# Banded attention and a mixture of experts in fp32: the second matrix product of the second pass from eight block products to seven

## The chip, the core and the metric

The kernel runs on one core of a Trainium2 chip. The metric is the device time of one execution in microseconds, the median of several runs. All data are float32. The matrix products use the one-pass float32 form (called F32R in the code) with every operand split into a high part, rounded to that form, and a low part (the rest): a product of two split operands is high x high, high x low and low x high, three matmuls.

## The reference

Attention over 4 batches, 8 heads, 576 positions of 64 values gives x, 2304 tokens of 512 values. Then the part that matters here, a dense mixture of 4 experts:

```python
def _moe_ref(x, domain_probs, w1, w2):          # x 2304x512, w1 4x512x1024, w2 4x1024x512
    p = domain_probs / (domain_probs.sum(-1, keepdims=True) + 1e-09)
    out = np.zeros((N, D), dtype=np.float32)
    for e in range(E):
        h = np.maximum(x @ w1[e], 0.0)
        out += p[:, e:e + 1] * (h @ w2[e])
    return out
```

## The kernel before

The hidden dimension of the experts is cut into 16 units of 256 values (4 of each expert), the tokens into 3 blocks of 768. A visit (u, m) works one unit on one block: the first product (x times the unit's 512 x 256 columns of w1), the relu, the second product (768 x 256 hidden values times the unit's 256 x 512 rows of w2), and an add into the block's accumulator, weighted with the token's share of that expert.

The first pass visits all units on block 0 while attention still makes blocks 1 and 2. The second pass is the list `visits` (lines 597 and 598): unit by unit, blocks 1 and 2, 32 visits. The weights of each unit are loaded again for it (`fetch_w1`, `fetch_w2`) and split again (`w1_split`, `w1_sums`, `w1_late`, `w2_late`; high parts on ScalarE, L130; low parts and differences mostly on GpSimd, L127 and L164 to L170).

The first product (`mm1_a`, `mm1_b`, matmuls at L475) already takes seven block products for a 2 x 2 block matrix (a Strassen form): A11, A12, A22 and S1 to S4 are blocks of w1 and sums of them, B11, B21, B22 and T1 to T4 those of x. A block product is 6 matmuls of 384 columns into one PSUM bank; ScalarE copies and VectorE adds put the four blocks of h together (L512 to L540), then h is split into a high part with relu (ScalarE, L493) and a low part (VectorE, L499).

The second product (`mm2`, matmuls at L579) is the plain one. For each of 6 tiles of 128 tokens it runs 6 matmuls of 512 columns with a block of h as the loaded (stationary) operand and w2 as the moving one. Then VectorE weighs the tile and adds it to the accumulator (L588). Three tiles go behind the opening block product of the next visit, three behind the one after that, so that VectorE and ScalarE work beside PE. In the last visit each tile is sent out (L593), the last one in two halves of 256 columns.

All instructions of an engine run in the order in which they are written. All the loads of weights, keys, queries and values and the outputs stand in one queue, SP's, in order too; a DMA that must wait for its buffer holds up what is behind it. `prepare`, `need` and `step` hand out the splitting work in small pieces between PE's work.

Of the kernel before, what the change touches and what calls it, by code (L numbers as in the profile page):

```python
# [48 lines left out]
def kernel(  # L49
# [30 lines left out]
    fp = ctx.enter_context(tc.tile_pool(name="fp", bufs=1))  # L80
    pools = {}
    wp = ctx.enter_context(tc.tile_pool(name="wp", bufs=1))

    ident = const.tile([128, 128], F32, name="ident")
    eps = const.tile([128, 1], F32, name="eps")
# [13 lines left out]
    w2_op = {}  # L99
    raw1 = {}  # L100
    raw2 = {}

    def fetch_w1(u, part=0):
        e, s = divmod(u % NU, FPE)
# [5 lines left out]
        src = w1[e, :, s * FU:(s + 1) * FU].rearrange("(c p) f -> p c f", p=128)  # L110
        nc.sync.dma_start(out=raw1[u][:, c], in_=src[:, c])

    def fetch_w2(u):
        e, s = divmod(u % NU, FPE)
        r = wp.tile([128, 2, DM], F32, tag="r2", name="r2")
        nc.sync.dma_start(
            out=r, in_=w2[e, s * FU:(s + 1) * FU, :].rearrange("(c p) d -> p c d", p=128)
        )
        raw2[u] = r

    held = []
# [13 lines left out]
    def w1_split(u):  # L135

        r = raw1[u]
        gh = wp.tile([128, 3, 2, 128], F32R, tag="g1h", name="g1h", bufs=2)
        gl = wp.tile([128, 3, 2, 128], F32R, tag="g1l", name="g1l", bufs=2)
        a11, a12 = r[:, 0:2, 0:128], r[:, 2:4, 0:128]  # L140
# [31 lines left out]

    def w1_late(u):
        r = raw1.pop(u)
        gh = wp.tile([128, 4, FU], F32R, tag="g2h", name="g2h")
        gl = wp.tile([128, 4, FU], F32R, tag="g2l", name="g2l")
        for n, c, f in (("S2", 0, 0), ("S1", 2, 128), ("S3", 0, 128), ("S4", 2, 0)):
            v = (slice(None), slice(c, c + 2), slice(f, f + 128))
            split(gh[v], gl[v], r[v], nc.gpsimd if u > 2 else nc.vector)
            a_op[u, n] = (gh[v], gl[v])  # L180
            yield
        if u + 2 <= LAST:
            fetch_w1(u + 2)

    def w2_late(u):
# [7 lines left out]
        if 1 < u < LAST:  # L193
            fetch_w2(u + 1)


    b_op = {}

# [350 lines left out]
    def plain(k, half):  # L549
# [4 lines left out]
        for i in range(2):  # L554
            for c in range(2):
# [2 lines left out]
                    h_out(k, f"{c + 1}{half + 1}", banks[c], 2 if (c, half) == (0, 0) else 1)  # L558
                yield "full"

    def mm2(k, first, last, half, cs=None):
        u, m = k
        e = u // FPE % E
        if first and m not in acc_t:
            if m == NBL - 1:
                pools["late"]()
            acc_t[m] = pools["acc"].tile([128, TB // 128, DM], F32, name=f"acc_{m}")
        for i in range(TH // 128):
            at = half * (TH // 128) + i
            tt = m * (TB // 128) + at  # L570
            acc = acc_t[m][:, at, :]
            cs = cs or (range(2) if half == 0 else (1, 0))
            split_tile = last and k == visits[-1] and half == 0 and i == TH // 128 - 1
            for d in (slice(0, DM // 2), slice(DM // 2, DM)) if split_tile else (slice(0, DM),):
                po = pools["m2"].tile([128, 512], F32, tag="m2", name="m2")[:, d]
                for n, (c, low) in enumerate([(c, low) for low in range(2) for c in cs]):
                    h = h_t[k, f"{c + 1}{half + 1}"][low][:, i * 128:(i + 1) * 128]
                    for x, w in enumerate(w2_op[u, c][:2 - low]):
                        nc.tensor.matmul(  # L579
                            po, h, w[:, d], start=(n == 0 and x == 0), stop=(n == 3)  # L580
                        )
                if first:
                    nc.vector.tensor_scalar(
                        out=acc[:, d], in0=po, scalar1=pn[:, tt, e:e + 1], scalar2=None,
                        op0=ALU.mult,
                    )
                else:
                    nc.vector.scalar_tensor_tensor(  # L588
                        out=acc[:, d], in0=po, scalar=pn[:, tt, e:e + 1], in1=acc[:, d],
                        op0=ALU.mult, op1=ALU.add,  # L590
                    )
                if last:
                    nc.sync.dma_start(out=out[tt * 128:(tt + 1) * 128, d], in_=acc[:, d])  # L593
            yield


    visits = [(u, 0) for u in range(2, NU)]
    visits += [(NU + u, m) for u in range(NU) for m in range(1, NBL)]

    def experts(begin):  # L600

# [31 lines left out]
        prepare(w1_split, 3)  # L633
        prepare(w1_sums, 3)
        prepare(w2_late, 3)
        for i, (u, m) in enumerate(visits):
            blocks = [b for v, b in visits if v == u]
            mine = [v for v in visits if v[1] == m]
            ends = m and (u, m) == mine[0], (u, m) == mine[-1]
            if m == blocks[0]:  # L640
                need(w1_late, u)
            yield from mm1_b((u, m))
            if m == blocks[-1] and u < LAST:
                prepare(w1_late, u + 1)
            if (u, m) == (NU - 1, 0):
# [3 lines left out]
            if m == blocks[-1] and u + 2 <= LAST:  # L649
                prepare(w1_split, u + 2)  # L650
                prepare(w1_sums, u + 2)
            if i + 1 < len(visits):

                need(w1_split, visits[i + 1][0])
                need_x(visits[i + 1][1], ("B11", "B21"))
                opening = mm1_a(visits[i + 1])
                yield next(opening)
            if m == blocks[0]:
                need(w2_late, u)
            yield from mm2((u, m), *ends, 1)  # L660
            if i + 1 < len(visits):
                begin()
                yield from opening
                if visits[i + 1] == (NU - 1, 0):

                    assert "m1" in gate
                    need(x_sums, 5)
                    for n in ("T2", "T1"):
                        for j in (4, 5):
                            prepare(x_part, j, n)  # L670
            yield from mm2((u, m), *ends, 0)
            if m == blocks[-1] and u + 2 <= LAST:
                prepare(w2_late, u + 2)

    queue = []
# [25 lines left out]
    with tc.manual_schedule():  # L703
# [3 lines left out]
        early = ExitStack()  # L707
        xrc = early.enter_context(ExitStack())
        psum = bass.MemoryType.PSUM
        pools["acc"] = fp  # L710
# [49 lines left out]
        def begin():  # L760

            if "over" in gate and "m1" not in gate:
                gate.add("m1")
                early.close()
                pools["x"] = ctx.enter_context(
                    tc.tile_pool(name="x2", bufs=1, side="right", reuse_waits="tile")
                )
                for n, bufs in ("m1", 2), ("m2", 4):
                    pools[n] = ctx.enter_context(
                        tc.tile_pool(name=n, bufs=bufs, space=psum, reuse_waits="tile")  # L770
                    )
                pools["acc"] = pools["x"]
# [31 lines left out]
        def x_over():  # L804
            for of in (queue, later):
                while any(key[0] in (x_part, x_sums) for key, _ in of):
                    step(of)
            xrp.__exit__(None, None, None)
            pools["acc"] = ctx.enter_context(
                tc.tile_pool(name="acc2", bufs=1, reuse_waits="tile")  # L810
            )

        pools["late"] = x_over
        gate = set()

        def pause(what):
# [252 lines left out]
```

## Time and profile before

| | |
|---|---|
| median of 3 runs | 824.52 us (822.99 to 825.04) |
| span of the profiled execution | 821.4 us |
| its own time | not listed apart; the median is 3.1 us above the span |
| granted TensorE clock | 1.000 (mean) |
| PE busy, VectorE busy | 812.7 us, 483.5 us |
| HBM read, written | 53.45 MB, 4.72 MB |

Times in rows are microseconds from the span's start unless marked ns. PE is TensorE's matmul, PEld its weight load, DVE VectorE, ACT ScalarE, POOL GpSimd, SP the engine whose queue issues the DMAs; a q behind a name means the engine's queue. L588 is line 588 of the kernel. A row of instructions says line, engine, operation, output<-inputs, shapes, count, then busy time and mean duration of one in ns, then idle time of the engine just before them and what ended it. Matmuls overlap in the pipeline, so the distance of their starts, not their duration, is what one costs.

### The profile page before, as it was taken

Reading aid. Unit: us, or ns where it says so; the run is one execution under the profiler, and the core shown is the slowest. Engines: PE = TensorE matmul, PEld = TensorE weight load, DVE = VectorE, ACT = ScalarE, POOL = GpSimd, SP = SyncE. Lnnn points to the kernel's source line nnn. Section 1 sums busy time; section 2 is a strip of 40 time slices with the busy share of each in tenths; the row PEclk is TensorE's granted clock in tenths of the full one; section 3 lists DMA queues with packets and bytes.
Section 4 is the critical chain, followed back from the end, with each engine's and each line's share of the span. In section 5 each row is a group of like instructions: output and inputs, shape, how many; then the busy total and the mean of one; then the engine's idle time right before and its main releaser. Section 6 shows DMA issues by size and latency. Waiting matters only on the chain.

```text
span 821.4 us, 15447 instructions
## 1 busy us (share of the span) xinstructions
PE 812.7 (99%) x6162; PEld 720.8 (88%) x6162; DVE 483.5 (59%) x1058; ACT 314.7 (38%) x749; POOL 390.3 (48%) x465
## 2 busy tenths in 40 slices
PE   8999999999999999999999999999999999999998
PEld 5778888888888889889889889889889989989987
DVE  5887557665765777555554554554554554555555
ACT  3554454544455446224223323323323323333321
POOL 4546878786777879334233233233243143153110
PEclk9999999999999999999999999999999999999999
DMA  7764624245211124110010010010010010010003
GB/s 230 230 180 132 193 71 133 83 128 158 91 53 52 52 92 140 35 43 26 26 51 27 26 52 26 26 52 26 27 52 26 26 52 26 27 51 1 1 26 128
DMA packets 46770, 59.15 MB, mean 72 GB/s; under 512 B 2905, under 2 KB 36313, under 8 KB 46699
## 3 DMA queue, kind: packets, MB, share of 16 engines
q1 hardware_dynamic: 46283, 57.75, 22.4%
q8 instruction: 48, 0.79, 0.4%
q10 hardware_dynamic: 416, 0.43, 0.1%
q14 instruction: 23, 0.19, 0.1%
HBM read 53.45 MB, written 4.72 MB: 71 GB/s over the span
## 4 chain that ended last, share of the span: by engine, by line
PE 92%; DVE 4%; DMA 1%; ACT 1%; issue 1%; POOL 0%; SPq 0%; POOLq 0%; DVEq 0%; ACTq 0%
PE m L579 46%; PE m1y L475 24%; PE m1x L475 18%; PE po L389 2%; DMA r<-w 1%; PE sc L300 1%; PE wt L824 1%; PE pt L369 1%; DVE xr L227 1%; DVE acc L588 1%; DVE sm L314 1%; DVE hl L499 0%; DVE su L345 0%; ACT hh L493 0%; DVE su L347 0%
## 5 line engine op out<-in xcount | busy, mean ns | idle before, releaser
L588 DVE SCALAR_TENSOR_TENSOR acc<-m,pn,acc 128x512 f32<-128x512 f32 (+1 forms) x271 | 202.2, 747 | 132.0 <-PE m L579 131.9
L579 PE MATMUL m<-w2h,hh 128*128 128x512 f32 x578 | 227.7, 394 | 0.8 <-DVE acc L588 0.3
L579 PE MATMUL m<-w2l,hh 128*128 128x512 f32 x578 | 225.5, 390 | 0.0
L127 POOL TENSOR_TENSOR g2l<-r,g2h 128x256 fp32r<-128x256 f32 x116 | 85.2, 759 | 235.0 <-PE m L579 212.7
L579 PE MATMUL m<-w2h,hl 128*128 128x512 f32 x578 | 179.0, 390 | 0.0
L493 ACT ACTIVATE hh<-s 128x384 fp32r<-128x384 f32 x92 | 48.3, 526 | 236.3 <-DVE s L516 185.2
L579 PEld LDWEIGHTS m<-w2h,hl 128*128 128x128 f32 x578 | 108.3, 188 | 24.5 <-DVE hl L499 1.0
L579 PEld LDWEIGHTS m<-w2h,hh 128*128 128x128 f32 x578 | 108.5, 188 | 23.2 <-DVE acc L588 2.6
L579 PEld LDWEIGHTS m<-w2l,hh 128*128 128x128 f32 x578 | 108.6, 188 | 19.5
L127 POOL TENSOR_TENSOR g1l<-r,g1h 128x256 fp32r<-128x256 f32 x93 | 70.0, 773 | 65.6 <-ACT g1h L130 65.6
L127 POOL TENSOR_TENSOR w2l<-r,w2h 128x512 fp32r<-128x512 f32 x58 | 75.2, 1315 | 47.1 <-ACT w2h L130 47.1
L535 DVE TENSOR_TENSOR s<-m1y,s 128x384 f32<-128x384 f32 x46 | 25.6, 556 | 93.8 <-PE m1y L475 92.3
L526 ACT ACTIVATE u<-m1y 128x384 f32<-128x384 f32 x46 | 22.6, 492 | 146.0 <-PE m1y L475 146.0
L499 DVE SCALAR_TENSOR_TENSOR hl<-s,hh 128x384 fp32r<-128x384 f32 x92 | 55.3, 601 | 27.7 <-ACT hh L493 27.5
L475 PE MATMUL m1y<-xh_T,g2h 128*128 128x384 f32 x152 | 51.9, 341 | 0.0
L475 PE MATMUL m1y<-xl_T,g2h 128*128 128x384 f32 x152 | 51.2, 337 | 0.0
L475 PE MATMUL m1y<-xh_T,g2l 128*128 128x384 f32 x152 | 51.0, 336 | 0.0
L130 ACT ACTIVATE g2h<-r 128x256 fp32r<-128x256 f32 x120 | 42.2, 407 | 0.8 <-POOL r L168 0.8
L475 PE MATMUL m1x<-xh_B,g2h 128*128 128x384 f32 x124 | 41.7, 337 | 0.0
L475 PE MATMUL m1x<-xl_B,g2h 128*128 128x384 f32 x124 | 41.7, 336 | 0.0
L475 PE MATMUL m1x<-xh_B,g2l 128*128 128x384 f32 x124 | 41.4, 334 | 0.0
L130 ACT ACTIVATE w2h<-r 128x512 fp32r<-128x512 f32 x64 | 38.3, 622 | 4.6 <-DMA r<-w 4.6
(133 smaller groups left out, 1477.2 us busy)
## 6 DMA issues: line engine op xcount, KB each, us to landing
r<-w SPq DMA_DIRECT2D x63, 512.0 KB, 3.3
v_s<-vw SPq DMA_DIRECT2D x48, 192.0 KB, 4.6
k_s<-kT SPq DMA_DIRECT2D x23, 224.0 KB, 4.8
q_s<-qT SPq DMA_DIRECT2D x24, 192.0 KB, 4.7
out<-acc SPq DMA_DIRECT2D x17, 256.0 KB, 2.0
r<-w SPq DMA_DIRECT2D x2, 256.0 KB, 4.3
out<-acc SPq DMA_DIRECT2D x2, 128.0 KB, 1.9
k_s<-kT ACTq DMA_DIRECT2D x1, 224.0 KB, 3.7
```

What stands on the lines that cost most here:

```text
L127: lo_eng.tensor_tensor(out=lo, in0=src, in1=hi.bitcast(F32), op=ALU.subtract)
L130: nc.scalar.activation(out=hi, in_=src, func=AF.Copy)
L227: nc.vector.tensor_tensor(out=quarter(i, d), in0=quarter(i, a), in1=quarter(i, b), op=ALU.subtract)
L300: nc.tensor.matmul(banks[swap][o:o + QB, i * KB:(i + 1) * KB], q_s[h, c0:c0 + QB], k_s[h, c0:c0 + KB], start=True, stop=True, skip_group_c ...
L389: nc.tensor.matmul(po[k][64 * j:64 * j + 64, o:o + QB], v_s[rows, j, 2 * i + half, :], ts_[rows, c:c + QB], start=True, stop=True,)
L475: nc.tensor.matmul(bank, w[:, k], x[:, k], start=(first and k == 0 and i == 0), stop=(last and k == 1 and i == 2), skip_group_check=True,)
L493: nc.scalar.activation(out=hi, in_=src, func=AF.Relu)
L499: nc.vector.scalar_tensor_tensor(out=lo, in0=src, scalar=0.0, in1=hi.bitcast(F32), op0=ALU.max, op1=ALU.subtract)
L526: nc.scalar.activation(out=u2, in_=x, func=AF.Copy)
L535: nc.vector.tensor_tensor(out=s5, in0=x, in1=s5, op=ALU.add)
L579: nc.tensor.matmul(po, h, w[:, d], start=(n == 0 and x == 0), stop=(n == 3))
L588: nc.vector.scalar_tensor_tensor(out=acc[:, d], in0=po, scalar=pn[:, tt, e:e + 1], in1=acc[:, d], op0=ALU.mult, op1=ALU.add,)
```

## The change

The second pass is written anew. Two units of the same expert form a pair, and a group is a pair on one block (16 groups, pairs (2,3), (4,5), ... (14,15), (0,1), blocks 1 and 2 in turn). The pair's h is a 2 x 2 block matrix (halves of the block's tokens by units) and its w2 one too (units by halves of the 512 outputs), so the second product takes seven block products P1 to P7 of 384 x 256 by 256 x 256. Each is 3 tiles of 128 tokens, a tile 6 matmuls of 256 columns. The products add up in two running sums in PSUM, x (P1, P6, P7, P4) and y (P5, P3, then P2 alone); after each product its 3 tiles are weighed into the accumulator's half.

The sums S1 to S4 of h blocks are made on VectorE, then split (`hi` on ScalarE, `lo` on VectorE, 768 columns each). Those of w2 are made by GpSimd once per pair (`w2_parts`, one step behind each of the seven places of a group). The seven split operands of each unit's first weights are written to DRAM in the first pass (`keep_w1`, units 2 to 15; `w1_again` makes those of units 0 and 1 in the background from group 3 on), and each is loaded (256 KB) when the visit before has used the one in its place (`load_w1`). In time, the second product of a group stands between the block products of the next group's first product. The first group has the six last tiles of the first pass there instead, and the last group's second product has nothing beside it.

The core of the diff:

```diff
-    LAST = 2 * NU - 1
+    LAST = NU - 1
+    def keep_w1(u):
+        kept[u] = dram.tile([NO, 128, 2, FU], F32, name=f"w1_{u}")
+        g1h, g1l, g2h, g2l = ready1.pop(u)
+        for side, tiles in enumerate(((g1h, g2h), (g1l, g2l))):
+            for at, t in zip((slice(0, 3), slice(3, NO)), tiles):
+                nc.sync.dma_start(
+                    out=kept[u][at, :, side, :].rearrange("n p f -> p n f"),
+                    in_=t.bitcast(F32).rearrange("p n c f -> p n (c f)"),
+                )
...
-    visits += [(NU + u, m) for u in range(NU) for m in range(1, NBL)]
...
+            need(w1_late, u)
+            keep_w1(u)
+            yield from mm1_b((u, 0))
...
+    PRODUCTS = (
+        ("A12", "B21"), ("A11", "B11"), ("S1", "T1"), ("S2", "T2"), ("S4", "B22"),
+        ("S3", "T3"), ("A22", "T4"),
+    )
...
+    PARTS = {
+        "P1": ("A11", "x", True, (0, 0)), "P5": ("S1", "y", True, (1, 1)),
+        "P6": ("S2", "x", False, (0, 1)), "P3": ("S4", "y", False, (0, 1)),
+        "P7": ("S3", "x", False, (1, 1)), "P2": ("A12", "y", True, (0, 0)),
+        "P4": ("A22", "x", False, (1, 0)),
+    }
...
+    def m1(g, i):
+        v, j = divmod(i, 7)
...
+        product(to, "s", n, g.m, b_, j < 3)
+        at = 2 * g.n + v + 1
+        if at < len(visits2):
+            load_w1(visits2[at][0], n)
+        if j == 0:
+            copy(out=g.h[v, 0][:, 0], in_=to, func=AF.Copy)
+        elif j == 1:
+            add(out=g.h[v, 0][:, 0], in0=to, in1=g.h[v, 0][:, 0], op=ALU.add)
+        elif j == 2:
+            copy(out=g.h[v, 1][:, 1], in_=to, func=AF.Copy)
+        elif j == 3:
+            copy(out=g.h[v, 1][:, 0], in_=to, func=AF.Copy)
+        elif j == 4:
+            add(out=g.h[v, 1][:, 0], in0=to, in1=g.h[v, 1][:, 0], op=ALU.add)
+        elif j == 5:
+            add(out=g.h[v, 1][:, 1], in0=to, in1=g.h[v, 1][:, 1], op=ALU.add)
+        else:
+            copy(out=g.h[v, 0][:, 1], in_=to, func=AF.Copy)
...
+    def m2(g, n):
+        factor, chain, begins, (i, j) = PARTS[n]
...
+        for t, to in enumerate(tiles):
+            ops = [(low, c, x) for low in range(2) for c in range(2) for x in range(2 - low)]
+            for k, (low, c, x) in enumerate(ops):
+                nc.tensor.matmul(
+                    to, h_places[factor][low][:, c, t * 128:(t + 1) * 128], w[:, x, c],
+                    start=begins and k == 0 and t != 1, stop=k == len(ops) - 1,
+                    skip_group_check=True,
+                )
...
+        for t, po in enumerate(tiles):
...
+            weigh_out(acc_t[g.m][:, at, d], po, tt, g.e, g.first and n in FIRST)
+            if g.last and n in ("P3", "P7", "P2", "P4"):
+                nc.sync.dma_start(
...
+    def w2_parts(pair):
+        raw = []
+        for u in pair:
+            r = pools["late"].tile([128, 2, DM], F32, tag="r", name="r", bufs=2)
+            nc.sync.dma_start(out=r, in_=w2_rows(u))
+            raw.append(r)
+        yield
...
+        def split2(n, src):
+            h, l = w2s[n][:, 0], w2s[n][:, 1]
+            nc.scalar.activation(out=h, in_=src, func=AF.Copy)
+            nc.gpsimd.tensor_tensor(out=l, in0=src, in1=h.bitcast(F32), op=ALU.subtract)
+        tt = nc.gpsimd.tensor_tensor
+        split2("P1", b11)
+        yield
+        tt(out=b11, in0=b12, in1=b11, op=ALU.subtract)
+        split2("P5", b11)
+        yield
+        tt(out=b11, in0=b11, in1=b22, op=ALU.subtract)
+        split2("P6", b11)
+        yield
+        split2("P3", b22)
+        yield
+        tt(out=b12, in0=b22, in1=b12, op=ALU.subtract)
+        split2("P7", b12)
...
+            def background(b):
+                q, odd = divmod(n, 2)
+                if n == 0:
+                    if b == 3:
+                        w2_steps = w2_parts(pairs2[0])
+                        next(w2_steps)
+                    for _ in range(2 if b > 2 else 0):
+                        next(w2_steps, 0)
+                elif odd and b == 2 and q + 1 < len(pairs2):
+                    w2_steps = w2_parts(pairs2[q + 1])
+                    next(w2_steps)
+                elif not odd and b > 0 or odd and b < 2:
+                    next(w2_steps, 0)
+                if n > 2 and again and next(again[0], 0) == 0:
+                    again.pop(0)
```

The order of one round, g the new group and h the one before (`mm1(i)` is block product i of g, 0 to 6 of its first unit and 7 to 13 of its second; `mm2_(b)` is the b-th of P1, P5, P6, P3, P7, P2, P4 of h):

```diff
+            of(h, hi, "S1"); mm1(0); of(h, lo, "S1"); of(h, h_sum, "S2"); mm2_(0); mm1(1); background(0)
+            of(h, hi, "S2"); mm1(2); of(h, lo, "S2"); of(h, h_sum, "S4"); mm2_(1); mm1(3); background(1)
+            of(h, hi, "S4"); of(h, lo, "S4"); mm1(4); mm2_(2); mm1(5); background(2)
+            mm1(7); of(h, hi, "A12"); of(h, lo, "A12")   ; relu of g.h[0, 1] on ScalarE
+            mm2_(3); of(h, hi, "A22"); of(h, lo, "A22"); mm1(6); background(3)
+            of(g, hi, "A11"); mm1(8); of(g, lo, "A11"); mm2_(4); mm1(9); background(4)
+            mm1(10); of(g, h_sum, "S3"); of(g, hi, "S3"); mm2_(5); mm1(11); background(5)
+            of(g, lo, "S3"); mm1(12); of(g, h_sum, "S1"); mm2_(6); mm1(13); background(6)
```

(In the file each call stands on a line of its own.)

## Rows read from the trace of the kernel before

**Rows 1.** The page, part 1: busy us (share of the span) x instructions.
```profile
PE 812.7 (99%) x6162; PEld 720.8 (88%) x6162; DVE 483.5 (59%) x1058; ACT 314.7 (38%) x749; POOL 390.3 (48%) x465
```

**Rows 2.** The chain of waits, two visits of the second pass: start, us, what.
```profile
468.12 4.12 PE m L579 x18
472.25 1.06 PE m1y L475 x6
473.31 4.12 PE m L579 x18
...
478.50 1.04 PE m1x L475 x6
...
499.26 4.12 PE m L579 x18
```

**Rows 3.** Groups of instructions by line and form, from 352 to 806 us.
```profile
L588 DVE SCALAR_TENSOR_TENSOR acc<-m,pn,acc 128x512 f32<-128x512 f32 x174 | 130.4, 749 | 93.9 <-PE m L579 93.9
...
L127 POOL TENSOR_TENSOR w2l<-r,w2h 128x512 fp32r<-128x512 f32 x28 | 35.7, 1292 | 42.1 <-ACT w2h L130 42.1
...
L493 ACT ACTIVATE hh<-s 128x384 fp32r<-128x384 f32 x58 | 30.5, 526 | 167.8 <-DVE s L516 132.0 <-DVE s L535 35.8
...
L130 ACT ACTIVATE w2h<-r 128x512 fp32r<-128x512 f32 x28 | 17.4, 620 | 0.0
...
L499 DVE SCALAR_TENSOR_TENSOR hl<-u,hh 128x384 fp32r<-128x384 f32 x29 | 16.2, 558 | 3.6
L516 DVE TENSOR_TENSOR s<-m1y,s 128x384 f32<-128x384 f32 x29 | 16.2, 558 | 10.7 <-PE m1y L475 10.7
...
L526 ACT ACTIVATE u<-m1y 128x384 f32<-128x384 f32 x30 | 14.8, 492 | 109.2 <-PE m1y L475 109.2
```

**Rows 4.** The timeline of the kernel's end: start, us, engine, line, what.
```profile
816.60 0.28 PE L579 MATMUL m<-w2h,hh 128*128 128x256 f32 x1
816.60 0.19 PEld L579 LDWEIGHTS m<-w2l,hh 128*128 128x128 f32 x1
...
816.71 0.19 PEld L579 LDWEIGHTS m<-w2h,hh 128*128 128x128 f32 x1
...
817.79 0.40 PE L579 MATMUL m<-w2h,hl 128*128 128x256 f32 x2
818.23 0.48 DVE L588 SCALAR_TENSOR_TENSOR acc<-m,pn,acc 128x256 f32<-128x256 f32 x1 [0.23 <-PE m L579]
```

**Rows 5.** The page, part 6, DMA issues: KB each, median us from issue to landing.
```profile
r<-w SPq DMA_DIRECT2D x63, 512.0 KB, 3.3
...
out<-acc SPq DMA_DIRECT2D x17, 256.0 KB, 2.0
```

**Rows 6.** The timeline of SP in the first pass (DMA issues).
```profile
184.83 0.37 SPq L111 DMA_DIRECT2D r<-w  x1
...
189.03 1.19 SPq L285 DMA_DIRECT2D v_s<-vw  x2
```

**Rows 7.** The timeline of ScalarE in the same stretch.
```profile
195.33 0.42 ACT L130 ACTIVATE g2h<-r 128x256 fp32r<-128x256 f32 x1
```

**Rows 8.** Busy time by stretch: us, each engine (x instructions), PEclk, DMA share, GB/s.
```profile
180.00:196.00 16.00, 15.85 (x181) 13.52 (x168) 10.21 (x42) 8.56 (x23) 11.44 (x14) 1.00 0.53 163
...
308.00:324.00 16.00, 16.00 (x83) 14.52 (x82) 11.83 (x17) 9.64 (x24) 14.73 (x16) 1.00 0.38 123
...
818.00:821.40 3.40, 0.19 (x2) 0.00 (x0) 0.48 (x1) 0.00 (x0) 0.00 (x0) 0.90 0.44 154
```

**Rows 9.** Groups by line and form over the whole span, VectorE.
```profile
L499 DVE SCALAR_TENSOR_TENSOR hl<-u,hh 128x384 fp32r<-128x384 f32 x46 | 32.8, 713 | 4.4
```

**Rows 10.** The timeline, all engines, one low part beside GpSimd.
```profile
294.71 0.74 POOL L166 TENSOR_TENSOR r<-r 128x256 f32<-128x256 f32 x1
...
294.93 0.93 DVE L499 SCALAR_TENSOR_TENSOR hl<-s,hh 128x384 fp32r<-128x384 f32 x1
```

**Rows 11.** The chain of waits at the turn of the passes.
```profile
311.32 1.05 PE m1x L475 x6
```

More of the change, by code (lines that the diff above doesn't have):

```diff
@@ L572, in mm2 @@
             cs = cs or (range(2) if half == 0 else (1, 0))
[L573 to L593, printed above, removed]
+            po = pools["m2"].tile([128, 512], F32, tag="m2", name="m2")
+            for n, (c, low) in enumerate([(c, low) for low in range(2) for c in cs]):
+                h = h_t[k, f"{c + 1}{half + 1}"][low][:, i * 128:(i + 1) * 128]
+                for x, w in enumerate(w2_op[u, c][:2 - low]):
+                    nc.tensor.matmul(po, h, w, start=(n == 0 and x == 0), stop=(n == 3))
+            weigh_out(acc, po, tt, e, first)
+            if last:
+                nc.sync.dma_start(out=out[tt * 128:(tt + 1) * 128], in_=acc)
             yield
     visits = [(u, 0) for u in range(2, NU)]
-    visits += [(NU + u, m) for u in range(NU) for m in range(1, NBL)]
     def experts(begin):
@@ L635, in experts @@
         prepare(w2_late, 3)
[L636 to L645, printed above, removed]
+        for i, (u, _) in enumerate(visits):
+            end = u == LAST
+            need(w1_late, u)
+            keep_w1(u)
+            yield from mm1_b((u, 0))
+            if end:
                 for n in ("T3", "T4"):
@@ L658, in experts @@
[L658 to L671, printed above, removed]
@@ L672, in experts @@
-            if m == blocks[-1] and u + 2 <= LAST:
-                prepare(w2_late, u + 2)
+            need(w1_split, u + 1)
+            opening = mm1_a((u + 1, 0))
+            yield next(opening)
+            need(w2_late, u)
+            yield from mm2((u, 0), False, False, 1)
+            begin()
+            yield from opening
+            if u + 1 == LAST:
+                assert "m1" in gate
+                need(x_sums, 5)
+                for n in ("T2", "T1"):
+                    for j in (4, 5):
+                        prepare(x_part, j, n)
@@ new lines, in experts @@
+            yield from mm2((u, 0), False, False, 0)
+            if u + 2 <= LAST:
+                prepare(w2_late, u + 2)
+        need(w2_late, LAST)
+        ends = [mm2((LAST, 0), False, True, half) for half in (1, 0)]
+        yield from second_pass(tile for half in ends for tile in half)
+    PRODUCTS = (
+        ("A12", "B21"), ("A11", "B11"), ("S1", "T1"), ("S2", "T2"), ("S4", "B22"),
+        ("S3", "T3"), ("A22", "T4"),
+    )
+    KEPT = ("A11", "A12", "A22", "S2", "S1", "S3", "S4")
@@ new lines, with w1_places, load_w1 @@
+    pairs2 = [(u, u + 1) for u in range(2, NU, 2)] + [(0, 1)]
+    groups = [(pair, m) for pair in pairs2 for m in range(1, NBL)]
+    visits2 = [(u, m) for pair, m in groups for u in pair]
+    w1s = {}
+    def w1_places(pool, names):
+        for n in names:
+            w1s[n] = pool.tile([128, 2, 2, 128], F32R, name=f"s_{n}")
+            a_op["s", n] = (w1s[n][:, 0], w1s[n][:, 1])
+    def load_w1(u, n):
+        nc.sync.dma_start(
+            out=w1s[n].bitcast(F32).rearrange("p s c f -> p (s c f)"),
+            in_=kept[u][KEPT.index(n)].rearrange("p s f -> p (s f)"),
+        )
@@ new lines, in h_sum @@
+    def h_sum(g, n):
+        one, two, to, op = {
+            "S3": ((0, 0), (0, 1), None, ALU.subtract),
+            "S1": ((1, 1), (0, 1), (0, 1), ALU.add),
+            "S2": ((0, 0), "S1", (0, 0), ALU.subtract),
+            "S4": ((1, 0), "S2", (0, 1), ALU.add),
+        }[n]
+        if to is None:
+            g.h[n] = pools["g"].tile([128, 2, TH], F32, tag="g", name="g", bufs=7)
+        else:
+            g.h[n] = g.h[to]
+        nc.vector.scalar_tensor_tensor(
+            out=g.h[n], in0=g.h[one], scalar=0.0, in1=g.h[two], op0=ALU.max, op1=op
+        )
@@ new lines, in w1_again @@
+    def w1_again(u):
+        r = pools["g"].tile([128, 4, FU], F32, tag="r1", name="r1")
+        nc.sync.dma_start(out=r, in_=w1_rows(u))
+        kept[u] = dram.tile([NO, 128, 2, FU], F32, name=f"w1_{u}")
+        yield
+        a11, a12 = r[:, 0:2, 0:128], r[:, 2:4, 0:128]
+        a21, a22 = r[:, 0:2, 128:256], r[:, 2:4, 128:256]
+        tt = nc.gpsimd.tensor_tensor
+        for n, src, one, two, op in (
+            ("A11", a11, None, None, None), ("A12", a12, None, None, None),
+            ("A22", a22, None, None, None), ("S1", a22, a21, a22, ALU.add),
+            ("S3", a21, a11, a21, ALU.subtract), ("S2", a11, a22, a11, ALU.subtract),
+            ("S4", a12, a12, a11, ALU.subtract),
+        ):
+            if op is not None:
+                tt(out=src, in0=one, in1=two, op=op)
+            t = pools["late"].tile([128, 2, 2, 128], F32R, tag="again", name="again")
+            nc.scalar.activation(out=t[:, 0], in_=src, func=AF.Copy)
+            tt(out=t[:, 1], in0=src, in1=t[:, 0].bitcast(F32), op=ALU.subtract)
+            yield
+            nc.sync.dma_start(
+                out=kept[u][KEPT.index(n)].rearrange("p s f -> p (s f)"),
+                in_=t.bitcast(F32).rearrange("p s c f -> p (s c f)"),
+            )
+            yield
```

239 lines of the change are left out of this document (208 added, 31 removed).

## The prediction

> **What bounds the kernel now.** I read the page's busy times first: PE is busy 99% of the span, VectorE 59%, GpSimd 48%, ScalarE 38% [rows 1]. A busy PE can still be waiting, so next came the chain of waits over two visits of the second pass: nothing but PE stands in it. Three tiles of the second product (18 matmuls) take 4.12 us, a block product of the first (6 matmuls) 1.04 to 1.06, and the pattern returns after 499.26 - 468.12 = 31.14 us [rows 2]. So there the time is the number of matmuls times their spacing, and 72 x 4.12 / 18 = 16.5 us of the 31.14 are the second product. Third, the groups of instructions of that stretch, for what the other engines pay per operation [rows 3]. Last, the timeline of the kernel's end, the only place where second-product matmuls of 256 columns run: their starts go from 816.60 to 817.79 in ten steps, 119 ns each [rows 4].
>
> **Term 1, the block product that goes.** A group replaces 2 x 36 matmuls of 512 columns by 7 products x 3 tiles x 6 = 126 matmuls of 256. Columns fall by an eighth, 36,864 to 32,256. Time falls less: 256 columns cost 119 ns where half of 229 would be 114.5. 126 x 0.119 = 15.0 us against 16.5, unrounded 1.47 a group, in 16 groups **-23.5 us**. The first product stays at 84 matmuls, 14.7 us, so a group takes 29.7. The weight splits that go from ScalarE and GpSimd give nothing: neither stands in the chain [rows 2].
>
> Each matmul still loads its own weights. The rows give a load 0.19 us, longer than the spacing, but the loads start 0.11 apart and so overlap [rows 4]. By the 119 ns spacing the term stands. The Trainium skill (Perfetto Trace Analysis, Identifying the Most-Contended Engine) has the reader judge TensorE's headroom by MFU and the busy share of the weight loads, not by matmul busy time. That share is 88% here [rows 1] and the change takes the loads of a pair of visits from 156 to 210: by that reading there is no room, and 210 x 0.188 = 39.5 us a group would be the sum's term. A last rival, below, is that case worked out from rows.
>
> **Term 2, the start of the second pass.** The first group has no second product beside it, only six old tiles of 1.37 us. Count from the end of the first pass's last first product. PE does seven block products (1.04) and six tiles and ends the seventh product of the first unit at 16.6. The two loads of second weights stand on SP behind the reload of that product's weights, which waits for it: issued at 16.8. A 512 KB load lands in 3.3 us [rows 5]; for two of them beside reloads and outputs I take 4.5: 21.3. ScalarE stands at the first high part and does nothing behind it. High part 0.62, GpSimd's low part 1.3 and difference 1.3, the second high part 0.62 [rows 3]: 25.2. Then the high part of A11 (768 columns) and the copy that PE needs: 26.6. PE could have gone on at 19.7: 7.0 us lost. The next copy stands behind two more splits: 2.0. The unit's last block product waits for an add right before it (1.35), S1's parts behind the last splits (1.2), smaller ones 0.8. Together **+12.3 us**; with the loads at 3.3 it is 11, without ScalarE in the way 1.4, with loads of 8 us 16. I take the first, since the place on SP and ScalarE's order are written out.
>
> The 768-column operations are estimates: VectorE takes 749 ns at 512 columns [rows 3] and 0.48 us at 256 [rows 4], 1.04 ns a column, so its 557 at 384 becomes 0.96 us at 768; ScalarE's 526 becomes 0.84 [rows 3].
>
> **Term 3, the tail.** The last group's second product stands alone. PE needs 15.0 us, VectorE 21 weighings x 0.48, five low parts and two sums x 0.96 = 16.8, and the products on S2 and S4 wait about 1.2 us each for their parts. I get 19.1 to the last weighing's end, 4.1 beyond PE's work, where the old end has 0.5 (818.19 to 818.71 [rows 4]). **+3.6 us**, bounds 1.5 and 6. Outputs leave in half widths, the last one right behind its weighing as now: 0.
>
> **Term 4, the other engines in the steady state: nothing.** VectorE has per group 6 adds x 0.557, 11 operations of 768 columns x 0.96, 21 weighings x 0.48: 3.3 + 10.5 + 10.1 = 24.0 of 29.7 us. Its order follows PE's; the tightest place is P4's weighing, done about 0.75 us after P4, before the next P1, with two block products (2.1 us) between. ScalarE has 8 copies x 0.49, 8 x 0.84 and 2.2 of splits, 12.8. Cover on VectorE 5.7 us a group; if it is gone, that is the second rival.
>
> **Term 5, the kept weights.** 14 units write 1.8 MB each in the first pass. Their four DMAs go to SP behind the last low part; today that place is 184.83, ahead of a burst of attention loads to 189 [rows 6]. The DMA share of that stretch is 0.53 at 163 GB/s [rows 8], so 1.8 MB want some 6 to 12 us. The next high part of these tiles is written at 195.33 [rows 7], over 10 us later. I take 0, bounds 0 and 14 x 1 us. In the second pass each reload has a visit, 15 us, to land 256 KB (an output of that size: 2.0 us [rows 5]): 0. Units 0 and 1, made again in groups 3 to 7, put GpSimd differences in front of ScalarE's high parts while a pair's splits run: some seven times 2 us of ScalarE, partly seen by PE: **+1.5 us**, bounds 0 and 6.
>
> **Term 6, the clock.** The granted clock is 1.00, and 0.90 in the mean over the last 3.4 us, in which PE stops at 818.2 [rows 8]: it fell to the 1.2 GHz level there. The 7 us of term 2 are a longer stop. If three block products and the next group's P1 then run at half speed, 5.3 us of work take twice as long, over half of it inside waits counted already: **+2 us**. No row shows how soon the clock comes back; bounds 0 and 5. The Trainium skill (TensorE: Matmul & The Clock Gate, Loop structure matters more than you think) warns of the same, a long wait between matmuls lets PE go cold.
>
> **Sum.** -23.5 + 12.3 + 3.6 + 0 + 0 + 1.5 + 2 = -4.1 us. The profiled execution has a span of 821.4; its own time is not listed; the median of the runs, 824.5, is 3.1 above the span, and what lies around the span does not change. So 817.3 of span, **820.4 us**. A measurement of this kernel can tell about 0.3% (2.5 us) from no change.
>
> **The rivals.**
> *The start costs little.* The loads land early or the copies get past the splits: term 2 at 1.4 and no clock loss give -23.5 + 1.4 + 3.6 + 1.5 = -17.0, 807.5 us; half of it, 814. For it: little else keeps ScalarE there. Against: the order of ScalarE and of SP. 0.18.
> *VectorE becomes the bound (slower).* Its low parts cost 713 ns for u over the whole span [rows 9], 558 in the second pass [rows 3], and one beside GpSimd 0.93 us [rows 10]. Its sum is 13.4 + 11 x, x the cost of a 768-column operation; it meets 29.7 at x = 1.48. Slowed by 713 / 558, x is 1.23; by 0.93 / 0.557, 1.6, and a group is 31.0, 1.3 longer. GpSimd has 11 operations x 1.3 = 14 us of splits per pair, most of them in every second group: 8 x 1.3 = 10.4, **831 us**; in all groups 841. The Trainium skill (SBUF — State Buffer, SBUF: two separate sides) says that VectorE with two SBUF inputs and GpSimd share a port pair under an exclusive lock; the 0.93 us of rows 10 agree. 0.15.
> *The kept weights slow the first pass (slower).* Held up by 1 us a visit, 14 us: 834. GpSimd is busy 11 to 15 us of 16 there [rows 8], so there is little room. 0.12.
> *Weight loads no longer hide (slower).* 126 x (0.188 - 0.119) = 8.7 us a group, 139 us: 960. Twelve matmuls speak against it [rows 4]. 0.02.
> That the change does not do what it says has no sign: the seven products close with their signs.
>
> **Chances.** My forecast 0.53, its own range 814 to 827. Faster by over 0.3% (under 822.0): the first rival and six tenths of the forecast, 0.5. Within: 0.22. Slower (over 827.0): the other rivals, 0.29, less the part of them that stays small, 0.28. The range takes in half of the first rival and the near ends of the slower ones: 810 to 833.
>
> **What would show it.** Right: in the second pass's chain 18 matmuls take 2.1 to 2.2 us and a group 29.7; PE idles 5 to 10 us once, some 20 us into the pass, behind ScalarE's split of second weights; the clock dips there only; VectorE ends the last PE waits. Wrong: a spacing over 125 ns in long runs of 256 columns; a wait for a weighing or a copy in every group; a last first product of the first pass that ends more than 2 us after today's 311.3 [rows 11].

## The result and the profile after

The changed kernel takes 833.01 us (median of 4 runs, 832.53 to 833.97) where the kernel before takes 823.91 beside it: a ratio of 1.0109, 95% interval 1.0095 to 1.0124. It is **slower by 1.1%**. The forecast was 820.4 us, faster. The profiled execution has a span of 832.2 us and its own time is 833.97, so 1.8 lie around the span.

The page of the changed kernel, first its parts 1 and 2, then the traffic and two of the new DMA groups (KB each, us from issue to landing):

```profile
PE 800.9 (96%) x7020; PEld 752.2 (90%) x7020; DVE 600.9 (72%) x1249; ACT 347.3 (42%) x707; POOL 368.0 (44%) x367
...
PE   8999799999999999599999999999999999999997
...
PEclk9999899999999999879999999999999999999999
...
HBM read 104.83 MB, written 34.08 MB: 167 GB/s over the span
...
s_S<-w SPq DMA_DIRECT2D x128, 256.0 KB, 2.9
...
w<-g2l SPq DMA_DIRECT2D x14, 512.0 KB, 6.2
```

Against [rows 1] PE has lost 12 us of busy time, and still the span is 10.8 longer. The two largest losses are holes that the slices show, the fifth slice (83 to 104 us) and the seventeenth (333 to 354 us). Both times the clock row dips with the PE row or right behind it.

The steady state is what was forecast. The chain of waits there, one round from P4 to P4 of the next (start, us, what):

```profile
601.08 2.16 PE x L825 x18
603.25 2.09 PE m1x L501 x12
605.34 2.15 PE x L825 x18
607.49 1.04 PE m1x L501 x6
...
630.81 1.30 PE x L825 x11
```

18 matmuls of 256 columns take 2.14 to 2.16 us (119 to 120 ns each), only PE stands in the chain, and the pattern returns after 630.81 - 601.08 = 29.73 us (from first product P1 to first product P1 the trace has 29.69 to 29.71 in nine of the 15 rounds) where [rows 2] has 31.14.

So where did the gain go? Each line below is read from the two profiled executions:

| part | forecast | measured | how it is read |
|---|---|---|---|
| block product that goes, 16 groups | -23.5 | -23.0 | 16 x (31.14 - 29.70) |
| start of the second pass, with its clock loss | +12.3 + 2 | +16.5 | end of the last first product of the first pass to P1: 39.5, work alone 15 x 1.045 + 3 x 2.76 = 24.0; next round 30.69, 1.0 too long |
| units 0 and 1 made again | +1.5 | +6.4 | rounds of 31.09, 31.46, 31.11, 31.50 for 29.70 |
| tail | +3.6 | +1.8 | P1 to the end 17.3, less 15.0 of work and the 0.5 of [rows 4] |
| first pass | 0 | +9.55 | its last first product ends, and the second pass starts, at 320.87, before at 311.32 [rows 11] |
| sum | -4.1 | +11.2 | span: +10.8 |

**The first pass.** Up to the load of a new unit's weights near 78 us the lag is 2.4 us (79.73 against 77.32 in the old kernel). Most of it goes with a short stretch of low clock at 17 to 21 us: in the trace of run 1 below, which has no such stretch, the lag there is 0.6 us (77.92). The stretch stands in some traces and not in others, and the mean clock of one kernel's executions varies too: the 27 executions of the kernel before in the second session run from 822.2 us at a mean clock of 1.000 to 827.9 at 0.992. Whether the change makes it more frequent was not tried. The rest, 7.1 us, arises at unit 2. The timeline of SP's queue there (start, us, instruction):

```profile
79.73 0.37 SPq L125 DMA_DIRECT2D r<-w  x1
80.14 0.51 SPq L218 DMA_DIRECT2D w<-g1h  x1
80.69 0.49 SPq L218 DMA_DIRECT2D w<-g2h  x1
81.23 1.03 SPq L218 DMA_DIRECT2D w<-g1l  x1
82.30 1.45 SPq L218 DMA_DIRECT2D w<-g2l  x1
83.79 4.02 SPq L311 DMA_DIRECT2D v_s<-vw  x4
...
90.01 0.41 SPq L129 DMA_DIRECT2D r<-w  x1
```

The same stretch of the kernel before:

```profile
77.32 0.37 SPq L111 DMA_DIRECT2D r<-w  x1
77.73 2.68 SPq L285 DMA_DIRECT2D v_s<-vw  x4
...
82.60 0.41 SPq L116 DMA_DIRECT2D r<-w  x1
```

and ScalarE there, with its wait for that last load in brackets:

```profile
88.22 1.15 ACT L130 ACTIVATE w2h<-r 128x512 fp32r<-128x512 f32 x2 [4.57 <-DMA r<-w]
```

Four writes (L218) stand between. They hold SP for 3.65 us of issuing, the four loads behind them are issued 1.3 us slower, and so the load of unit 2's second weights (the last line) goes out 10.3 us after the first line, where it was 5.3. What that does, in the waits of 86 to 104 us of the changed kernel (in total, times, longest):

```profile
ACT w2h L141 <- DMA r<-w: 9.5, 1, 9.5
POOL w2l L138 <- ACT w2h L141: 7.7, 1, 7.7
DVE hl L525 <- ACT hh L519: 5.9, 1, 5.9
...
PE m L612 <- DVE acc L593: 5.3, 1, 5.3
```

Read it downwards, one in-order engine after the other: ScalarE stands at the split of the late weights for 9.5 us; behind that split in its program is a high part of h (`hh`); VectorE waits for it to make the low part (`hl`), and behind that stand two weighings (`acc`) whose tiles PE had finished long before; PE, which needs their place in PSUM, stops for 5.3 us. ScalarE waited for this load in the kernel before as well, 4.57 us, and PE had no stop there: the 5.0 us by which the wait grew are about what PE stands still. The granted clock is at the low level, 1.2 GHz, for 6.8 us, from 96.2 to 103.0; 2.5 us of that lie in the stop and 4.3 behind it.

**The start of the second pass.** The loads of second weights land after 6.39 us, and the waits of 325 to 372 us read:

```profile
PE m1y L501 <- ACT g L763: 8.8, 1, 8.8
ACT w_P L855 <- DMA r<-w: 6.2, 1, 6.2
...
ACT w_P L855 <- POOL r L869: 2.9, 1, 2.9
ACT w_P L855 <- POOL r L861: 2.7, 1, 2.7
...
ACT w_P L855 <- POOL r L874: 2.4, 1, 2.4
```

It is the picture of term 2: PE waits once, long, for a copy (L763) that stands behind ScalarE's splits (L855), the first of which waits for the DMA and the later ones for GpSimd's differences. Two stretches of the windows then show the clock (us, PE busy ..., PEclk, DMA share, GB/s):

```profile
338.00:350.00 12.00, 3.19 (x18) 2.87 (x17) 1.45 (x2) 2.52 (x5) 4.02 (x4) 0.81 0.57 195
350.00:360.00 10.00, 7.86 (x24) 6.85 (x24) 6.65 (x6) 3.90 (x7) 8.52 (x6) 0.50 0.18 58
```

From 350 to 360 PE is busy for 7.86 of 10 us and granted 0.50, the 1.2 GHz level; the whole low stretch is 17.1 us, from 345.4 to 362.5, and its first 4.1 us lie in the stop.

**Units 0 and 1 made again.** In the four long rounds (450 to 575 us) PE waits four times, once in each, for an add of VectorE (L761); in total, times, longest:

```profile
PE m1x L501 <- DVE g L761: 5.0, 4, 1.5
```

The chain that leads to the second of these waits (start, us, what):

```profile
481.63 1.28 POOL w_P L856
482.91 0.70 POOL r L895
...
483.63 0.42 ACT again L897
484.05 0.74 ACT h0h L779
...
485.69 2.05 DVE g L807
487.74 1.18 DVE acc L593 x3
488.92 0.47 DVE g L761
...
489.43 1.31 PE m1x L501 x6
```

GpSimd's work for the pair (`w_P`) and for the remade unit (`r` L895) follow each other; ScalarE's split for the remade unit (`again` L897) waits for the latter, and the high part that VectorE needs (`h0h`) stands behind that split. VectorE's low part, the next sum, three weighings and the add come late in turn, and PE waits for the add, 1.45 us here.

### The profile page after: what moved, and what is told of

The parts are those of the page before. It is cut to its first block, busy times and chain, and to the rows that moved or that the text cites. A ratio compares the mean times of both kernels' runs of the same rounds, so it can differ in the third digit from the quotient of the medians.

```text
span 832.2 us, 17899 instructions
## 1 busy us (share of the span) xinstructions
PE 800.9 (96%) x7020; PEld 752.2 (90%) x7020; DVE 600.9 (72%) x1249; ACT 347.3 (42%) x707; POOL 368.0 (44%) x367
## 4 chain that ended last, share of the span: by engine, by line
PE 84%; POOL 5%; DVE 5%; issue 3%; ACT 2%; DMA 1%; DVEq 0%; POOLq 0%; SPq 0%; ACTq 0%
PE m1x L501 24%; PE m L612 15%; PE m1y L501 15%; PE x L825 14%; PE y L825 11%; PE po L415 2%; POOL w_P L856 2%; PE sc L326 2%; DMA r<-w 1%; DVE acc L593 1%; PE wt L1177 1%; PE pt L395 1%; DVE xr L253 1%; DVE g L807 1%; POOL r L895 1%
## 5 line engine op out<-in xcount | busy, mean ns | idle before, releaser
L856 POOL TENSOR_TENSOR w_P<-r,w_P 128x512 fp32r<-128x512 f32 x56 | 75.9, 1357 | 259.8 <-PE m1y L501 164.0
L593 DVE SCALAR_TENSOR_TENSOR acc<-m,pn,acc 128x512 f32<-128x512 f32 x90 | 67.1, 748 | 39.2 <-PE m L612 39.1
L612 PE MATMUL m<-w2h,hh 128*128 128x512 f32 x192 | 77.9, 406 | 5.5 <-DVE acc L593 5.5
L807 DVE SCALAR_TENSOR_TENSOR g<-g 128x768 f32<-128x768 f32 x64 | 78.1, 1220 | 0.5
L612 PE MATMUL m<-w2l,hh 128*128 128x512 f32 x192 | 75.7, 394 | 0.0
L593 DVE SCALAR_TENSOR_TENSOR acc<-x,pn,acc 128x256 f32<-128x256 f32 x174 | 73.0, 473 | 0.9 <-PE x L825 0.9
L501 PE MATMUL m1x<-xh_B,s_A 128*128 128x384 f32 x256 | 66.2, 340 | 0.0
L825 PE MATMUL x<-w_P,xh_T 128*128 128x256 f32 x384 | 61.5, 282 | 0.0
L612 PE MATMUL m<-w2h,hl 128*128 128x512 f32 x192 | 60.3, 395 | 0.4 <-DVE hl L525 0.4
L855 ACT ACTIVATE w_P<-r 128x512 fp32r<-128x512 f32 x56 | 34.9, 627 | 53.4 <-POOL r L861 21.1
L612 PEld LDWEIGHTS m<-w2h,hh 128*128 128x128 f32 x192 | 36.3, 189 | 14.9 <-DVE acc L593 7.6
```

The costliest lines, as they stand in the source:

```text
L501: nc.tensor.matmul(bank, w[:, k], x[:, k], start=(first and k == 0 and i == 0), stop=(last and k == 1 and i == 2), skip_group_check=True,)
L593: nc.vector.scalar_tensor_tensor(out=acc, in0=po, scalar=pn[:, tt, e:e + 1], in1=acc, op0=ALU.mult, op1=ALU.add,)
L612: nc.tensor.matmul(po, h, w, start=(n == 0 and x == 0), stop=(n == 3))
L807: nc.vector.scalar_tensor_tensor(out=g.h[n], in0=g.h[one], scalar=0.0, in1=g.h[two], op0=ALU.max, op1=op)
L825: nc.tensor.matmul(to, h_places[factor][low][:, c, t * 128:(t + 1) * 128], w[:, x, c], start=begins and k == 0 and t != 1, stop=k == len(o ...
L855: nc.scalar.activation(out=h, in_=src, func=AF.Copy)
```

## The experiments

My theory was that three losses, at unit 2, at the start and in the remade units, are each made by the **place** of a few instructions in an in-order queue, not by how much work or traffic was added. Eight kernels tested it, all measured beside the kernel before (medians of 824.55 and 823.58 us in the two sessions). Times of one kernel differ by up to 6.3 us between executions (822.12 to 828.38 in run 7), and its mean clock varies with them; so the traces decide the single us, and the medians the whole. The last run compares the two.

**1. keep_later.** The writes of every unit go behind `mm1_b`, the last five of the seven block products of its first product. (Where an expectation below says "first second-product part", this place is meant.)

```diff
-            keep_w1(u)
             yield from mm1_b((u, 0))
+            keep_w1(u)
```

> Every unit's four writes of kept weights go to SP behind the unit's first product instead of ahead of it. Theory (order on SP): in the changed kernel the first unit's writes push the second weights of unit 2 from 82.60 to 90.01 us, PE waits some 5 us at 93 to 98.7 and the clock drops for 6.8 us; behind the product the load goes out where it did, so about 7 us come back: 826, and no low clock before 300 us. Rival (volume): the 26 MB of writes crowd the DMA engines wherever they stand, so another load is late and the time stays within 2 us of 833.

Measured: 824.65 us, ratio to the kernel before 0.9997 (0.9981 to 1.0014), 8.4 us less than the change. SP's queue of this kernel:

```profile
77.92 0.37 SPq L125 DMA_DIRECT2D r<-w  x1
78.33 2.51 SPq L311 DMA_DIRECT2D v_s<-vw  x4
...
83.03 0.41 SPq L129 DMA_DIRECT2D r<-w  x1
83.49 0.47 SPq L218 DMA_DIRECT2D w<-g1h  x1
```

The load goes out 5.1 us after the first line again, ScalarE waits 4.2 us for it, PE does not stop for it, the clock stays at 1.00 up to the start of the second pass, and the first product of the second pass starts at 312.89 instead of 320.87 us. The same 25.7 MB (14 x 1.835) are written in the same pass, so the volume of the writes, the rival, is not what cost the time.

**2. keep_first_other_queue.** Unit 2's four writes stay at their place in the program, but ScalarE's queue issues them.

```diff
-                nc.sync.dma_start(
+                (nc.scalar if u == 2 else nc.sync).dma_start(
```

> Only unit 2's four writes leave SP's queue for ScalarE's, at the same place of the program. Theory (order on SP): the second weights of unit 2 go out near 83 again and the time falls by 4 to 7 us, 826 to 829; the writes still share the DMA engines with them, so the load lands in over 5.6 us. Rival (volume): the load lands as late as in the changed kernel (near 95.6 us), 833.

Measured: 828.51 us, 1.0040 (1.0023 to 1.0056), 4.5 us less than the change, about half of what keep_later gives. SP is freed of the four issues, but its next four loads take 5.05 us to issue instead of 2.51, and the load of second weights goes out at 87.55, not near 83, 8.6 us after its first line. It lands in 4.7 us, not in over 5.6, and ScalarE waits 3.7 us for it; the stop of PE behind it shrinks from 5.3 to 0.7 us. A new stop stands ahead of it, on ScalarE's side (ScalarE's timeline, then PE's wait):

```profile
79.22 2.21 ACTq L218 DMA_DIRECT2D w<-g2l  x1
81.47 0.49 ACT L552 ACTIVATE u<-m1y 128x384 f32<-128x384 f32 x1 [2.51 <-DVE rc L377]
...
PE m1y L501 <- ACT u L552: 1.7, 1, 1.7
```

The issue of the last write holds ScalarE's queue for 2.21 us, and the copy behind it (`u`), for which PE stops, starts as soon as it ends (the row names another wait, VectorE's `rc`, which ends at about the same time; which of the two held the copy was not tried). The clock is low from 82.6 to 86.0. So the forecast time came out, but only in part by its mechanism; and the writes can cost on either queue, by what stands behind them there.

**3. keep_only_unit_2_later.** As 1, for unit 2 alone; the other 13 units are written where the change has them.

```diff
-            keep_w1(u)
+            if u > 2:
+                keep_w1(u)
             yield from mm1_b((u, 0))
+            if u == 2:
+                keep_w1(u)
```

> Only unit 2's four writes go behind its first second-product part; those of units 3 to 15 stay where the change put them. If unit 2 alone loses time by its writes (the trace shows the loss once), this equals the run with all of them later: 824 to 827, the first product of the second pass starting near 314 us. If the others cost some too and only hide it behind unit 2's, it stays above that by 1 us or more: 827 to 831.

Measured: 826.36 us, 1.0017 (0.9998 to 1.0036). The interval overlaps that of run 1, so the medians alone can't tell the last 2 us; the trace agrees with the first reading: the first product of the second pass starts at 311.5 us, 1.4 earlier than in run 1. The 13 other units' writes cost nothing that shows in it; only at unit 2 is there no slack.

**4. start_load_earlier.** The two loads of second weights for the first group go to SP as soon as the first pass lets their buffers go; the splits stay.

```diff
                     first_over()
+                    load_pair()
...
-                    if b == 3:
-                        w2_steps = w2_parts(pairs2[0])
-                        next(w2_steps)
```

> Only the load of pair 0's second weights is issued earlier, right after the first products of the first pass are over; the splits stay at places 3 to 6 of the first group, two at a place. If the late landing of the load (6.2 us of ScalarE's wait) made the loss at the start, most of the 11.5 us come back: 820 to 824. If the crowding of the splits into four places, ahead of the copies that TensorE waits for on ScalarE, made it, 829 to 832.

Measured: 827.82 us, 1.0045 (1.0026 to 1.0064), 5.2 less than the change. From the last first product of the first pass to P1 it takes 35.0 us (39.5 without the edit), the next round 30.08. ScalarE's wait for the DMA falls from 6.2 to 1.7 us; PE still waits 4.3 us for the copy L763, and the clock still falls. The time lies between the two ranges of the expectation: neither cause makes the loss alone.

**5. start_splits_spread.** Only the splits move.

```diff
-                    for _ in range(2 if b > 2 else 0):
+                    for _ in range(b > 3):
+                        next(w2_steps, 0)
+                elif n == 1 and b < 2:
+                    for _ in range(2):
                         next(w2_steps, 0)
```

> Only the splits are moved: one each at places 4, 5 and 6 of the first group, two each at the first two places of the second. The load stays at place 3, behind the reload on its queue. If the late landing made the loss, little comes back since the first split still waits behind it on ScalarE: 829 to 833. If the crowding made it, 820 to 824. In between, 824 to 829, both have a share.

Measured: 824.37 us, 1.0000 (0.9982 to 1.0019), 8.6 less than the change. 29.4 us to P1, the next round 32.29. PE's longest wait in that stretch is 2.1 us. The two causes overlap: 5.2 + 8.6 is more than both together give, next. Spreading the splits gives the larger part, but this does not part the causes cleanly: the first split stands one place later too, and ScalarE's wait for the DMA falls from 6.2 to 2.5 us by that.

**6. start_splits_later.** Edits 4 and 5 together (the seven splits stand at five places, as in run 5).

> At the start of the second pass the loads of the first pair's second weights are issued as soon as their place is free (before three more reloads instead of behind them), and the seven splits are spread over seven later places instead of two at each of four. Theory (ScalarE stands at a split and PE's copies stand behind it): the PE wait of the stretch 340 to 356 us falls from 16.6 us of loss (clock included) to 3 to 6, so 820 to 823, with no low clock near 350. Rival (the chain of splits itself is too long for the first group): the wait moves to P5 to P4 of the next group, time 828 to 833.

Measured: 821.46 us, 0.9960 (0.9941 to 0.9979), 11.5 less than the change. 26.3 us to P1, the next round 32.58. The windows of this kernel show PE at work through the stretch and the clock at full level:

```profile
338.00:350.00 12.00, 10.16 (x63) 9.55 (x62) 7.41 (x8) 6.79 (x13) 7.07 (x5) 1.00 0.87 296
350.00:360.00 10.00, 9.56 (x65) 9.07 (x64) 7.84 (x11) 2.97 (x6) 7.93 (x5) 1.00 0.35 106
```

**7. again_apart.** Steps of the remade units only in odd rounds from the second place on, where of a pair's second weights only one split and the loads stand.

```diff
-                if n > 2 and again and next(again[0], 0) == 0:
+                if n > 2 and odd and b and again and next(again[0], 0) == 0:
```

> Units 0 and 1 are made again only in groups with an odd number, where GpSimd and ScalarE have no split of second weights to do. Theory (GpSimd's differences for units 0 and 1 between the pair's splits hold up ScalarE, and through it VectorE and PE in groups 4 and 6): the 6.3 us that these two groups lose against 29.7 come back, 826.5 to 828. Rival (the remaking costs DMA, GpSimd time or port time wherever it stands): the loss spreads over the odd groups, 831 to 834.

Measured: 824.85 us, 1.0003 (0.9984 to 1.0023). All rounds between the first and the last take 29.69 to 29.71, the four long ones too, which is 6.4 us; the rest of the 8.2 by which the median is lower is not explained by the edit (the short low clock near the start was absent in the profiled execution). The chain from 449 to 482 us, the first of the rounds that were long, names PE alone, and PE has no wait from 440 to 576 us:

```profile
by line: PE m1x L501 34.8%; PE x L825 32.0%; PE y L825 19.4%; PE m1y L501 14.2%
```

The remaking itself is all there; only its meeting with the pair's splits is gone.

**8. all_three_moved.** Edits 1, 4, 5 and 7 in one kernel; the whole computation is done.

> The keeping of every unit behind the first second-product part, the load of pair 0's second weights ahead and its splits spread and later, and remaking in odd groups alone, all at once; nothing is left out of the computation. If the three losses are independent, each made by the place of its instructions, the gains add: 833.0 less 6.9 (first pass at unit 2), less 11.5 (start), less 6.4 (remaking), so 806 to 810, below the kernel before by about 2 per cent; the first product of the second pass starts near 313 us, the group periods are all near 29.7. If they overlap (the wait in the first pass only moved idle time that the start would have had, or spreading the splits needs the slack of the place that the keeping took), 812 to 817. If the single runs were helped by the missing dip at the kernel's start, 809 to 812.

Measured: 809.72 us (808.28 to 812.10, 5 runs), ratio to the kernel before 0.9816 (0.9787 to 0.9845). It beats both kernels: by 23.3 us the changed one, and by 1.5 to 2.1% the one before. Its page:

```profile
PE 792.1 (98%) x7020; PEld 745.2 (92%) x7020; DVE 601.1 (74%) x1249; ACT 348.3 (43%) x707; POOL 370.2 (46%) x367
...
PE   8999999999999999999999999999999999999997
...
PEclk9999999999999999999999999999999999999999
```

Same instruction counts on every engine as in the changed kernel, no hole and no dip. The traces add up: the first product of the second pass starts at 313.13 (7.7 earlier), P1 follows after 26.3 instead of 39.5 (13.2), the rounds after it have 1.9 more once and 6.4 less in four: 7.7 + 13.2 - 1.9 + 6.4 = 25.4, and the last weighing ends 25.4 us earlier. The single losses, each read from the traces, are 7.1 + 11.3 + 6.4 = 24.8. So in the traces the three add up, to within 1 or 2 us: this trace also lacks the low clock at 17 to 21 us, some 1.8 of the 25.4, and without that 23.6 are left, near the 23.3 of the medians. The medians of the single runs do not add up so well: 8.4 + 11.5 + 8.2 = 28.1, and 809.72 lies in the range of independent losses (806 to 810) and at the low end of the one for single runs helped by a missing dip (809 to 812). That the losses sit where the edits are is shown; that they are independent to the last us is not.

## Why the prediction was wrong

**The step that failed first is term 5**, "I take 0" for the kept weights in the first pass. The prediction followed the writes to their buffers (when the next high part needs them) and asked how long 1.8 MB take. It looked at one place of the first pass, 184.83 [rows 6], and there the step holds: run 3 shows no cost of 13 of the 14 units. What it did not do is ask, for each place where the four writes are put, what stands behind them on SP and how late that already was. At unit 2 a load that ScalarE was already waiting 4.57 us for stood there, and that cost 7.1 us. The prediction's own sign of being wrong, a last first product that ends more than 2 us after 311.3, is what came: 9.55.

The rival of the kept weights had the right total, 834, by luck and for another reason: 1 us at each of 14 units by traffic and GpSimd. Run 1 leaves the traffic and takes the loss away, so that rival is not what happened.

**Second, the remaking of units 0 and 1**: forecast 1.5 of bounds 0 to 6, measured 6.4. The mechanism named (GpSimd differences ahead of ScalarE's high parts while a pair's splits run) is the one in the chain; its size came from taking PE to see a part of seven waits of 2 us. PE lost about 1.6 in each of four rounds, by way of VectorE, whose low part waits for the high part behind ScalarE's split.

**Third, term 2 and term 6 together**: 14.3 forecast, 16.5 measured. The mechanism was right in its main steps: the place on SP, ScalarE in the way, the one long wait of PE (7.0 forecast, 8.8 measured), the dip of the clock, which began in it. The mis-sized term is the landing of the loads, taken as 4.5 us between bounds of 3.3 and 8; it was 6.39. (The 16.6 us at which the reload is free need eight block products, not the seven that the text counts; the trace has 16.7.)

Together with the 2.4 us of lag that go mostly with the early low clock, the errors are 7.1 + 4.9 + 2.2 + 2.4 on the slow side, 0.5 in term 1 and -1.8 in the tail: 15.3, the distance from -4.1 to +11.2.

**What held.** Term 1: 119 to 120 ns a matmul, a round 29.7 us as forecast, and no wait of PE in its list of waits from 560 us to the tail. Term 4: VectorE is busy 23.73 of 30 us there, forecast 24.0 of 29.7; its 768-column operations take 0.95 us in their fastest groups and 1.19 in the mean from 560 to 806 us, inside the 1.48 from which it would have decided. So VectorE as the bound did not happen. The tail cost less than forecast, 1.8 for 3.6: PE waits in it only twice for a low part of h, 0.4 and 0.3 us.

**Weight loads.** In the steady state the windows show (PE, then PEld busy, of 30 us):

```profile
600.00:630.00 30.00, 30.00 (x214) 30.00 (x213) 23.73 (x40) 11.59 (x19) 6.46 (x5) 1.00 0.53 158
```

The loads of weights are busy all of the time, 213 of 189 ns each (40 us of loads in 30), and yet matmuls of 256 columns follow each other after 119 ns. So the loads overlap with each other in the records, and the rival that they no longer hide, given 0.02, fell. The prediction weighed a reading of the Trainium skill (Perfetto Trace Analysis, Identifying the Most-Contended Engine): TensorE's headroom is judged by MFU and the busy share of the weight loads. Taken as a limit on the number of loads, as the prediction did, that would have made the second product longer; the trace does not agree.

**The sign.** Without the losses of place, term 1 leaves 23 us, and run 8 keeps 14 of them. The forecast's "faster" rested on two sums that were taken at or near their lower bounds (0 of 0 to 14 for the kept weights, 1.5 of 0 to 6 for the remaking). The time came out at the edge of the range, 833.01 for 833.0, because the errors of the start and of both these sums point the same way; only the tail's points the other.

## What to carry to other kernels

When a change adds DMAs or small steps to an in-order queue, list for each place where they are put the next instruction on that queue that somebody waits for, and read from the old trace how long that somebody already waits: a wait that PE does not see yet is slack that is used up, and the next 5 us on that queue are PE's. Two background jobs that both go back and forth between ScalarE and GpSimd should not be stepped at the same places; apart from each other they cost nothing that shows, together 1.6 us a round. And a change that loses may hold a gain: here the arithmetic saved what it should, and moving four small pieces of the program turned +1.1% into about -1.8%.

## What the runs showed of the hardware that was not expected

**A stop of PE costs more than its length.** The granted clock went to the 1.2 GHz level within the stop of 8.8 us and within the one of 5.3 us at unit 2, and stayed there behind them, while PE worked again (columns as in the windows above):

```profile
349.50:362.50 13.00, 10.86 (x35) 9.84 (x36) 7.15 (x6) 4.93 (x9) 10.62 (x9) 0.50 0.24 81
98.70:103.00 4.30, 4.29 (x11) 3.71 (x12) 1.36 (x2) 0.00 (x0) 3.88 (x6) 0.50 0.36 124
```

Half of PE's busy time there, 5.4 and 2.1 us, is an estimate of what the low level cost: the stops cost about 1.6 and 1.4 times their length. Shorter stops were followed by it too: in run 5 a wait of 2.1 us, work of 1.3 us and a wait of 0.96 (low from 343.6 to 350.4 us), in run 2 a wait of 1.7 us (low from 82.6 to 86.0). In run 8 the longest wait in the start of the second pass was 1.0 us and the clock stayed at 1.00.

**Issuing is not free, and not constant.** One write of 384 to 512 KB held SP's queue for 0.36 to 1.45 us, and one of them ScalarE's for 2.21 us in run 2. Four loads of values took SP 2.51 and 2.68 us without such writes about, 4.02 us right behind four of them, and 5.05 us in run 2, where they went out beside it on ScalarE's queue; what makes them slower was not tried.

**The second pass has room in the DMA queues.** HBM traffic went from 58 MB to 139 MB, the DMA engines were busy for 0.53 of the time from 600 to 630 us, and PE waited for no reload of 256 KB (2.9 us to land in the median) in the steady state.
